# Eight more attention slots in the first batches; the second weight in four column groups, and the first half's output made one tile at a time

## The chip, the core and the metric

The kernel runs on one core of a Trainium2 chip. Time is the device time of one execution in microseconds (us). Five engines work side by side, each through its own queue in order: PE (TensorE, matrix products; PEld is its loading of the stationary operand), DVE (VectorE), ACT (ScalarE), POOL (GpSimd) and SP (SyncE, which here only issues transfers). A matrix product writes into PSUM, and DVE and ACT read it from there.

## What is computed

Causal attention with an extra bias for 8 batches of 8 heads (576 positions, head size 64), and behind it a feed-forward network over the 4608 tokens (512 to 2048 to 512):

```python
scores = scale * np.matmul(q, k.transpose(0, 1, 3, 2))
cum = np.cumsum(np.maximum(s, 0.0), axis=-1)
bias = -(cum[:, :, :, None] - cum[:, :, None, :])
scores = np.where(causal, -1000000000.0, scores + np.minimum(bias, 0.0))
attn = np.exp(scores - np.max(scores, axis=-1, keepdims=True))
attn = attn / (np.sum(attn, axis=-1, keepdims=True) + 1e-09)
x = np.matmul(attn, v)            # [B, H, S, D], then tokens x (H*D)
h = x @ w_in
g = np.where(h >= 1, h, np.where(h <= -1, 0.0, (h + 1) ** 2 / 4))
out = g @ w_out
```

The two weights come as 64-bit integers that hold doubles; the kernel decodes each to a 32-bit float, scales it by a power of two, and splits it into two 16-bit floats (a high and a low part). Every FFN product is then three 16-bit products.

## The kernel before

**Attention.** Work goes in jobs: a job is one pair of heads and one half of the positions. Half 0 (`hf` 0) has 320 positions in three row tiles (64, 128 and 128 rows), half 1 has 256 in two. A batch has eight jobs: four pairs of half 0, then four pairs of half 1. A job has eight slots (`att_slot(j, k)`, line 467): slot 0 converts q and k (`att_prep`), slots 2 to 7 make six units of scores (`scores`, lines 384 and 385 on PE, 390 on DVE, 401 on ACT), slot 3 issues the next job's loads on SP, and slot 7 makes the output of the job *before* (`att_out`, line 447 on PE, 458 and 459 for `x`). The weights of a row tile are split on POOL, ACT and DVE (lines 422 to 428) and transposed by a DMA on SP (line 429, tile `pt`); line 447 reads `pt`. The score tiles share two PSUM buffers.

**FFN.** A half of a batch goes through 16 row tiles of `w_in` (`ffn_h`, line 501: twelve products, three for each of four `kt`, where `kt` is the pair of heads), then ACT, DVE and POOL make `g` (lines 513 to 528), and `ffn_y` (line 540) adds each `g` into four output tiles `y0` to `y3` in PSUM, two row tiles behind. So the first product with `kt` = 3 needs the `x` of the last pair.

**Order.** The loop at line 605 has 512 steps, 32 for each half of a batch (two for each row tile). Each step issues one attention slot; in the first 32 steps every fourth step issues two. So from step 32 on, the slot counter `t` is 40 ahead of the step: step 32*q begins the FFN of half q (counted over all batches), and the `x` of its last pair comes from slot 32*q + 39, which was issued one step earlier. Attention ends 32 steps before the loop. A planner then sorts the instructions of each engine by priority (the order of issue, with leads of 6000 or 10000 for blocks under `high_priority`) and by its own simulated times; PE executes what it wrote strictly in that order.

**The second weight.** `Weights` (line 164) loads 16 chunks of 512 KB on SP (line 184), decodes each (lines 192 to 203), takes one scale over a group of chunks (`scale`, lines 208 to 216: ten small DVE instructions in a chain, with two PE products, lines 107 and 117, that use score buffers in PSUM) and splits the chunks (lines 221 to 229). For `w_out` there are two groups of eight chunks: 256 output columns each, a chunk being 256 rows by 256 columns. `w2_tasks` (line 591) issues two decode or split tasks at each of the first steps, with a lead of 6000. In steps 0 to 15 the FFN of the very first half only makes `h` and `g`; in steps 16 to 31 (lines 623 to 625) it makes `y`: first tiles 0 and 1 over all row tiles, then tiles 2 and 3, since the second group of `w_out` comes later. `batch_y` (line 294) makes one output scale per group and batch.

Of the kernel before, what the change touches and what calls it, by code (L numbers as in the profile page):

```python
# [14 lines left out]
AF = mybir.ActivationFunctionType  # L15
ALU = mybir.AluOpType
# [6 lines left out]
P = 128  # L23
NPAIR = H // 2
NKT = DM // P
NFT = DFF // P
# [25 lines left out]
WO_LAG = 2  # L52
# [21 lines left out]
def attention_ffn(ctx: ExitStack, tc: tile.TileContext, qT, kT, vT, s, w_in, w_out, yT):  # L74
    nc = tc.nc
    LOADQ, CUMQ, FIRSTQ = nc.sync, nc.scalar, nc.sync
    V, A, G, T = nc.vector, nc.scalar, nc.gpsimd, nc.tensor

    cp = ctx.enter_context(tc.tile_pool(name="cp", bufs=1))
    ap = ctx.enter_context(tc.tile_pool(name="ap", bufs=2))  # L80
    gp = ctx.enter_context(tc.tile_pool(name="gp", bufs=2))
# [75 lines left out]
    NC = 512  # L157
    WI = [cp.tile([P, 2, NC], F16, name=f"WI{c}") for c in range(NW)]
    WO = [cp.tile([P, 2, NC], F16, name=f"WO{c}") for c in range(NW + WO_LAG)]
# [4 lines left out]
    class Weights:  # L164
# [9 lines left out]
        def load(self, c, after=None):  # L174
            if c < NW:
                pool, tag, bufs = self.tags[c % len(self.tags)]
                self.raw[c] = pool.tile([P, NC, 2], I32, tag=tag, bufs=bufs, name=f"{self.name}r{c}")
                if after is not None:
                    V.tensor_copy(self.raw[c][:, 0, :1], after.bitcast(I32))
                src = self.src(c)  # L180
                dst = self.raw[c]
                if len(src.shape) == 4:
                    dst = dst.rearrange("p (j n) t -> p j n t", j=2)
                nc.sync.dma_start(dst, src)

        def decode(self, c):
# [46 lines left out]
        WO, WI, ((gp, "g", G_BUFS),), 1,  # L233
    )
    w2 = Weights(
        "wo", lambda c: w_out[c % 8 * 2 * P:(c % 8 + 1) * 2 * P, c // 8 * NC // 2:(c // 8 + 1) * NC // 2, :]
        .rearrange("(j p) n t -> p j n t", p=P),
        WO[WO_LAG:], WO, ((ap, "raw", 2), (gp, "x0", 2), (ap, "raw", 2)), 2,
    )
    a_in, b_out = w1.bound[0], w2.bound  # L240

# [1 line left out]
    vraw, csc, rcs, exs, hsc, rsc, usc, wsc, ubi, gsc, ysc, msc = ({} for _ in range(12))  # L243
# [25 lines left out]
    def batch_scales(b):  # L269
        m = msc[b]  # L270
        h = hsc[b] = ap.tile([P, 1], F32, tag="hs", name=f"hs{b}")
        V.tensor_scalar(h, m, a_in, 2.0 ** -27, ALU.mult, ALU.mult)

        r = rsc[b] = ap.tile([P, 1], F32, tag="r", name=f"r{b}")
        i = r.bitcast(I32)
        V.tensor_scalar(r, m, a_in, 2048.0, ALU.mult, ALU.mult)
        V.tensor_scalar(r, r, 1.0, None, ALU.max)
        V.reciprocal(r, r)
        V.tensor_scalar(r, r, 2.0 ** 14, None, ALU.mult)
        V.tensor_scalar(i, i, 23, None, ALU.logical_shift_right)  # L280
        V.tensor_scalar(i, i, 127, None, ALU.add)
        V.tensor_scalar(i, i, 1, 23, ALU.logical_shift_right, ALU.logical_shift_left)

        u = usc[b] = ap.tile([P, 1], F32, tag="us", name=f"us{b}")
        V.tensor_scalar(u, h, r, None, ALU.mult)
        w = wsc[b] = ap.tile([P, 1], F32, tag="ws", name=f"ws{b}")
        V.tensor_scalar(w, u, 2.0, None, ALU.mult)
        c = ubi[b] = ap.tile([P, 1], F32, tag="ub", name=f"ub{b}")
        V.tensor_scalar(c, r, 0.5, None, ALU.mult)
        g = gsc[b] = ap.tile([P, 1], F32, tag="gb", name=f"gb{b}")  # L290
        V.reciprocal(g, r)
        V.tensor_scalar(g, g, g, 2.0 ** 14, ALU.mult, ALU.mult)

    def batch_y(b, groups=(0, 1)):
        ysc.setdefault(b, {})
        for i in groups:
            y = ysc[b][i] = ap.tile([P, 1], F32, tag=f"ys{i}", name=f"ys{b}_{i}")
            V.tensor_scalar(y, gsc[b], b_out[i], 2.0 ** -28, ALU.mult, ALU.mult)
# [168 lines left out]
    def att_slot(j, k):  # L467

        if j < len(jobs):
            n, hf = jobs[j]  # L470
            if k == 0:
                att_prep(n, hf)
            if k == 1 and hf == 0:
                v_prep(n)
            if k == V_K and hf == 0:
                v_turn(n)
            if k >= 2:
                scores(n, *UNITS[hf][k - 2])
            if k == 3 and j + 1 < len(jobs):
                att_load(*jobs[j + 1])  # L480
            if k == 1 and j % (2 * NPAIR) == V_J and j // (2 * NPAIR) + 1 < B:
                load_v(j // (2 * NPAIR) + 1)
            if k == 5 and j + 1 < len(jobs) and jobs[j + 1][0] % NPAIR == 0 and jobs[j + 1][1] == 0:
                with tc.issue_after(ttr[0]):
                    batch_start(jobs[j + 1][0] // NPAIR)
        if k == OUT_K and 1 <= j <= len(jobs) and j != NPAIR:
            while j == len(jobs) and late:
                late.pop(0)()
            att_out(*jobs[j - 1])


    ffn_q, g4 = [], [None]
# [30 lines left out]
    def g_split(first=None):  # L523
        while to_split:
            g, u = to_split.pop()
            with tc.issue_after(first) if first is not None else ExitStack():
                A.copy(g[:, 0], u)  # L527
            G.tensor_tensor(g[:, 1], u, g[:, 0], ALU.subtract)  # L528

    ys = {}  # L530

    def ffn_y(b, hf, ft, g, ms=tuple(range(NKT))):
        h_off, N, _ = HALF[hf]
        if ft == 0:
            for m in ms:
                ys[b, hf, m] = ps_y.tile([P, 512], F32, tag=f"y{m}", name=f"y{b}_{hf}_{m}")
        for m in ms:
            c0 = ft % 2 * 2 * P + m % 2 * P
            for n, (wl, gl) in enumerate(((0, 0), (1, 0), (0, 1))):
                T.matmul(  # L540
                    ys[b, hf, m][:, :N], WO[8 * (m // 2) + ft // 2][:, wl, c0:c0 + P], g[:, gl],
                    start=(ft == 0 and n == 0), stop=(ft == NFT - 1 and n == 2),
                )
        if ft == NFT - 1:
            last = (b, hf) == (B - 1, len(HALF) - 1)
            for m in ms:
                tag, bufs = ("u", 4) if last and m >= 2 else ("o", O_BUFS)
                o = gp.tile([P, N], F32, tag=tag, bufs=bufs, name=f"o{b}_{hf}_{m}")
                y = ys[b, hf, m][:, :N]
                with tc.high_priority(offset=FFN_LEAD):  # L550
                    if last and m % 2:
                        V.tensor_scalar(o, y, ysc[b][m // 2], None, ALU.mult)
                    else:
                        A.activation(o, y, AF.Copy, scale=ysc[b][m // 2])
                (nc.sync if last and m % 2 else nc.scalar).dma_start(
                    yT[m * P:(m + 1) * P, b * S + h_off:b * S + h_off + N], o
                )

    def ffn_step(s, k):

        b, hf, ft = s // (2 * NFT), s // NFT % 2, s % NFT
        if k == 0:
            ffn_q.append((b, hf, ft, ffn_h(b, hf, ft)))
        elif len(ffn_q) > Y_LAG:
            ffn_y(*ffn_q.pop(0))
# [7 lines left out]
    for j in range(NPAIR):  # L573
        for k in range(8):
            if k % 2 == 0:
                c = 4 * j + k // 2
# [9 lines left out]
    for n in range(NW):  # L586
        c = n % 4 * 4 + n // 4
# [1 line left out]
    att_out(*jobs[NPAIR - 1])  # L589

    def w2_tasks():
        for g in range(2):
            for c in range(8 * g, 8 * g + 8):
                w2.decode(c)
                w2.load(c + 3)
                yield
            w2.scale(g, TINY)
            batch_y(0, (g,))
            for c in range(8 * g, 8 * g + 8):
                w2.split(c)  # L600
                yield

    t = 8 * NPAIR
    tasks = w2_tasks()
    for j in range(16 * NP):
        if j % 64 == 48 and j // 64 + 1 < B:
            batch_scales(j // 64 + 1)
            batch_y(j // 64 + 1)
        for _ in range(1 if j >= 2 * NFT else 1 + (j % 4 == 3)):
            att_slot(t // 8, t % 8)  # L610
            t += 1
        with tc.high_priority(offset=W2_LEAD):
            for _ in range(W2_RATE):
                next(tasks, None)
        if j >= 2 * NFT:
            ffn_step(j // 2, j % 2)
        elif j < NFT:
            ffn_step(j, 0)
        else:
            if j == NFT:  # L620
                with tc.high_priority(offset=FFN_LEAD):
                    g_split()
            m = 2 * (j // 8 % 2)
            for i in range(j % 8 * 2, j % 8 * 2 + 2):
                ffn_y(*ffn_q[i], ms=(m, m + 1))
            if j == 2 * NFT - 1:
                del ffn_q[:NFT]
    with tc.high_priority(offset=FFN_LEAD):
        g_split()
    while ffn_q:  # L630
        ffn_y(*ffn_q.pop(0))
# [28 lines left out]
```

## Time and profile before

| | us |
|---|---|
| median of 3 runs | 1171.36 (1170.36 to 1180.07) |
| the profiled execution | 1178.29 |
| its span, first to last instruction | 1176.2 |
| PE / DVE / ACT / POOL busy | 1009.5 / 892.6 / 746.0 / 691.0 |

The mean granted clock of PE is 0.967 of full speed. A busy PE is not a PE at its peak: matrix products are pipelined, and at a lower granted clock the same products are busy for longer. The table of stretches that is used below has, for each stretch of time, the busy time of PE, PEld, DVE, ACT and POOL with their instruction counts, then PE's granted clock, the share of the DMA engines and GB/s. A stretch's length less PE's busy time is PE's idle time.

### The profile page before, as it was taken

What the parts mean: (1) busy time and instruction counts of PE and PEld (TensorE: products, weight loads), DVE (VectorE), ACT (ScalarE), POOL (GpSimd) and SP (SyncE); (2) the same over time, 40 slices, a digit from 0 to 9 for tenths busy, and PEclk for the clock granted to TensorE, in tenths of its full rate; (3) what the DMA queues carried; (4) which work ended last, traced back from release to release, by engine and by line L of the source; (5) the groups of instructions that cost most, each with busy time, mean ns of one, the idle gap of its engine ahead of it and who ended that gap; (6) DMA issues with size and microseconds to landing.
All of it is one profiled execution on the core that took longest, in us unless ns stands there. A gap on an engine that the chain in (4) does not pass through costs nothing.

```text
span 1176.2 us, 25135 instructions
## 1 busy us (share of the span) xinstructions
PE 1009.5 (86%) x8470; PEld 776.6 (66%) x8470; DVE 892.6 (76%) x2404; ACT 746.0 (63%) x1719; POOL 691.0 (59%) x1169
## 2 busy tenths in 40 slices
PE   0234678699999999799998999899989999899998
PEld 0122345487767867587767867677768867686787
DVE  6879998778777877768777777778778877787633
ACT  4656677567656765767557665667557764777533
POOL 3876268676556664656546654656557564675522
PEclk9997999799998999999999999899999999899999
DMA  8885536867637773776638672876547753767310
GB/s 243 206 195 138 165 85 145 159 139 153 130 73 180 147 148 74 166 139 144 131 84 168 152 149 65 173 142 156 119 98 172 153 133 75 163 132 157 74 34 19
DMA packets 343081, 158.04 MB, mean 134 GB/s; under 512 B 291112, under 2 KB 324264, under 8 KB 342952
## 3 DMA queue, kind: packets, MB, share of 16 engines
q1 hardware_dynamic: 333248, 146.50, 59.0%
q10 hardware_dynamic: 9704, 9.93, 2.7%
q8 instruction: 67, 1.10, 0.4%
q14 instruction: 62, 0.51, 0.1%
HBM read 75.33 MB, written 9.73 MB: 72 GB/s over the span
## 4 chain that ended last, share of the span: by engine, by line
PE 42%; DVE 8%; DMA 5%; POOL 5%; issue 3%; ACT 1%; DVEq 0%; ACTq 0%; POOLq 0%
PE y L540 18%; PE h L501 17%; DMA pt<-pb 4%; PE px L447 3%; POOL pb L422 2%; DVE pb L428 2%; PE s L384 2%; PE s L385 2%; DMA vt<-vb 2%; POOL pb L425 1%; DVE p L390 1%; DVE K L339 1%; DVE h L516 1%; DVE Q L336 1%; POOL vb L350 1%
## 5 line engine op out<-in xcount | busy, mean ns | idle before, releaser
L501 PE MATMUL h<-x,WI 128*128 128x256 f16 (+1 forms) x3072 | 453.0, 292 | 23.4 <-DVE u L517 21.0
L540 PE MATMUL y<-g,WO 128*128 128x256 f16 (+1 forms) x3072 | 453.2, 291 | 17.3 <-POOL g L528 7.4
L501 PEld LDWEIGHTS <-WI 128*128 128x128 f16 x3072 | 292.3, 100 | 118.2 <-issue 28.2
L540 PEld LDWEIGHTS <-WO 128*128 128x128 f16 x3072 | 287.1, 99 | 108.7 <-issue 19.3
L528 POOL TENSOR_TENSOR g<-u,g 128x320 f16<-128x320 f32 (+1 forms) x256 | 199.2, 778 | 209.1 <-ACT g L527 203.9
L513 ACT ACTIVATE u<-h,ub,us 128x320 f32<-128x320 f32 (+1 forms) x256 | 149.3, 584 | 171.8 <-PE h L501 146.7
L401 ACT ACTIVATE p<-p,mn 64x64 f32<-64x64 f32 (+4 forms) x320 | 178.8, 559 | 113.6 <-DVE mn L390 96.4
L516 DVE SCALAR_TENSOR_TENSOR h<-h,ws,u 128x320 f32<-128x320 f32 (+1 forms) x256 | 133.0, 520 | 118.4 <-ACT u L513 117.9
L422 POOL TENSOR_SCALAR pb<-p,rs 64x128 f16<-64x128 f32 (+4 forms) x160 | 113.7, 711 | 152.2 <-DVE rs L418 118.6
L384 PE MATMUL s<-K,Q 128*128 128x288 f32 (+4 forms) x384 | 150.9, 395 | 43.8 <-DVE mn L390 33.3
L428 DVE SCALAR_TENSOR_TENSOR pb<-p,rs,pb 64x128 f16<-64x128 f32 (+4 forms) x160 | 135.8, 849 | 52.0 <-POOL pb L422 51.6
L425 POOL TENSOR_TENSOR pb<-p,pb 64x128 f16<-64x128 f32 (+4 forms) x160 | 165.0, 1032 | 9.2
L390 DVE CUSTOM_DVE_ANT_0 p<-s,mask 64x64 f32<-64x64 f32 (+4 forms) x320 | 134.8, 422 | 41.1 <-PE s L385 36.7
L517 DVE SCALAR_TENSOR_TENSOR u<-u,r,h 128x320 f32<-128x320 f32 (+1 forms) x256 | 130.2, 510 | 7.5
L423 ACT ACTIVATE p<-p,rs 64x64 f32<-64x64 f32 (+4 forms) x160 | 89.3, 559 | 67.2 <-DVE rs L418 60.6
L385 PE MATMUL s<-K,Q 68*128 68x288 f32 (+4 forms) x384 | 121.8, 319 | 9.8 <-ACT p L423 5.5
L447 PE MATMUL px<-pt,vt 128*64 128x256 f16 (+3 forms) x1536 | 87.7, 260 | 38.0 <-DMA pt<-pb 21.8
L384 PEld LDWEIGHTS s<-K,Q 128*128 128x128 f32 (+1 forms) x384 | 74.3, 194 | 68.2 <-DVE mn L390 42.4
L527 ACT CAST g<-u 128x320 f16<-128x320 f32 (+1 forms) x256 | 108.1, 422 | 10.6 <-DVE u L517 10.6
L447 PEld LDWEIGHTS <-vt 128*64 128x64 f16 x1536 | 73.2, 113 | 61.5 <-issue 40.3
L424 POOL TENSOR_SCALAR pb<-p 64x128 f16<-64x128 f32 (+4 forms) x160 | 90.9, 569 | 6.0 <-ACT p L423 2.9
L385 PEld LDWEIGHTS s<-K,Q 68*128 68x128 f32 (+1 forms) x384 | 75.8, 198 | 12.2 <-ACT p L423 5.9
(116 smaller groups left out, 961.4 us busy)
## 6 DMA issues: line engine op xcount, KB each, us to landing
rk<-in_k_dram SPq DMA_DIRECT2D x64, 288.0 KB
rq<-in_q_dram SPq DMA_DIRECT2D x64, 160.0 KB
rk<-in_k_dram SPq DMA_DIRECT2D x64, 160.0 KB
v<-in_v_dram SPq DMA_DIRECT2D x32, 288.0 KB
wir<-in_moe_w_in_dram SPq DMA_DIRECT2D x16, 512.0 KB
rq<-in_q_dram SPq DMA_DIRECT2D x64, 128.0 KB
wor<-in_moe_w_out_dram SPq DMA_DIRECT2D x16, 512.0 KB
out_dram<-o ACTq DMA_DIRECT2D x32, 160.0 KB
```

What stands on the lines that cost most here:

```text
L384: T.matmul(sc[:R, :c1 - c0], Q1[:, hd, qo:qo + R], K1[:, hd, c0:c1], start=True, stop=False)
L385: T.matmul(sc[:R, :c1 - c0], Q2[:KC, hd, qo:qo + R], K2[:KC, hd, c0:c1], start=False, stop=True)
L390: ttr[0] = V.tensor_tensor_reduce(out=Pt[:R, c0:c1], in0=sc[:R, :c1 - c0], in1=mask[:R, mo:mo + c1 - c0], scale=1.0, scalar=3.0e38 if mn i ...
L401: A.activation(Pt[:R, :W], Pt[:R, :W], AF.Exp, bias=m2[:R], scale=-1.0, accum_out=sums[n, i][:R, hd:hd + 1])
L425: G.tensor_tensor(los[1], pw, his[1], ALU.subtract)
L428: V.scalar_tensor_tensor(los[0], pv, rs[:R, :1], his[0], ALU.mult, ALU.subtract)
L447: T.matmul(px[hd * D:(hd + 1) * D, lo:N], VT[:, vl * NB + j, hd * D:(hd + 1) * D], PT[:, 4 * j + 2 * hd + pl, lo:], start=(m == 0), stop=( ...
L501: T.matmul(h[:, :N], WI[4 * kt + ft // 4][:, wl, ft % 4 * P:(ft % 4 + 1) * P], x[:, kt, xl], start=(n == 0), stop=(n == 3 * NKT - 1),)
L513: first = A.activation(u, h[:, :N], AF.Relu, bias=ubi[b], scale=usc[b]).ins
L516: V.scalar_tensor_tensor(h[:, :N], h[:, :N], wsc[b], u, ALU.mult, ALU.max)
L528: G.tensor_tensor(g[:, 1], u, g[:, 0], ALU.subtract)
L540: T.matmul(ys[b, hf, m][:, :N], WO[8 * (m // 2) + ft // 2][:, wl, c0:c0 + P], g[:, gl], start=(ft == 0 and n == 0), stop=(ft == NFT - 1 an ...
```

## The change

Three edits. First, `w_out` is cut into four groups of four chunks; a chunk is now 512 rows by 128 columns, so a group is exactly one output tile, each with its own scale, and `scale` and `batch_y` run for four groups. A contiguous run in memory is 128 columns of 8 bytes (1 KB) in place of 256 (2 KB). Second, the first half's `y` is made tile by tile: steps 16 to 19 make tile 0 over all 16 row tiles, 20 to 23 tile 1, and so on; each step has twelve products as before. Third, in steps 32 to 95 every eighth step issues one more attention slot, eight in all, so that from step 92 on the slot counter is 48 ahead of the step, and attention ends 40 steps before the loop.

```diff
@@ load
-                    dst = dst.rearrange("p (j n) t -> p j n t", j=2)
+                    dst = dst.rearrange("p (j n) t -> p j n t", j=src.shape[1])
@@ w2 = Weights(
-        "wo", lambda c: w_out[c % 8 * 2 * P:(c % 8 + 1) * 2 * P, c // 8 * NC // 2:(c // 8 + 1) * NC // 2, :]
+        "wo", lambda c: w_out[c % 4 * NC:(c % 4 + 1) * NC, c // 4 * P:(c // 4 + 1) * P, :]
         .rearrange("(j p) n t -> p j n t", p=P),
-        WO[WO_LAG:], WO, ((ap, "raw", 2), (gp, "x0", 2), (ap, "raw", 2)), 2,
+        WO[WO_LAG:], WO, ((ap, "raw", 2), (gp, "x0", 2), (ap, "raw", 2)), NKT,
@@ batch_y
-    def batch_y(b, groups=(0, 1)):
+    def batch_y(b, groups=range(NKT)):
@@ ffn_y
-            c0 = ft % 2 * 2 * P + m % 2 * P
+            c0 = ft % 4 * P
...
-                    ys[b, hf, m][:, :N], WO[8 * (m // 2) + ft // 2][:, wl, c0:c0 + P], g[:, gl],
+                    ys[b, hf, m][:, :N], WO[4 * m + ft // 4][:, wl, c0:c0 + P], g[:, gl],
...
-                        V.tensor_scalar(o, y, ysc[b][m // 2], None, ALU.mult)
+                        V.tensor_scalar(o, y, ysc[b][m], None, ALU.mult)
...
-                        A.activation(o, y, AF.Copy, scale=ysc[b][m // 2])
+                        A.activation(o, y, AF.Copy, scale=ysc[b][m])
@@ w2_tasks
-        for g in range(2):
-            for c in range(8 * g, 8 * g + 8):
+        for g in range(NKT):
+            for c in range(4 * g, 4 * g + 4):
                 w2.decode(c)
...
-            for c in range(8 * g, 8 * g + 8):
+            for c in range(4 * g, 4 * g + 4):
                 w2.split(c)
@@ the loop of steps
-        for _ in range(1 if j >= 2 * NFT else 1 + (j % 4 == 3)):
+        for _ in range(1 + (j % 4 == 3 if j < 2 * NFT else j % 8 == 3 and j < 6 * NFT)):
...
-            m = 2 * (j // 8 % 2)
-            for i in range(j % 8 * 2, j % 8 * 2 + 2):
-                ffn_y(*ffn_q[i], ms=(m, m + 1))
+            for i in range(j % 4 * 4, j % 4 * 4 + 4):
+                ffn_y(*ffn_q[i], ms=(j // 4 % 4,))
```

## The prediction

> **What bounds the kernel now.** I read the page first, then a table of stretches, then PE's timeline where PE is idle. The page's slices:
>
> ```profile
> PE   0234678699999999799998999899989999899998
> PEclk9997999799998999999999999899999999899999
> ```
>
> A slice is 29.4 us. The first eight (to about 235 us) have a partly idle PE; from then on PE is near full, with a dip about every 130 us, one for each batch. The stretches (after the times: PE, PEld, DVE, ACT, POOL busy; clock; DMA share; GB/s):
>
> ```profile
> 98.00:145.00 47.00, 24.91 (x133) 15.13 (x132) 43.41 (x97) 30.60 (x52) 22.46 (x24) 0.78 0.45 127
> 145.00:182.00 37.00, 27.34 (x189) 17.69 (x187) 33.68 (x74) 27.73 (x50) 24.79 (x24) 0.95 0.39 97
> 182.00:231.00 49.00, 36.01 (x267) 25.72 (x267) 40.46 (x112) 32.65 (x72) 36.27 (x55) 0.82 0.76 153
> 231.00:344.00 113.00, 110.56 (x956) 85.95 (x956) 86.28 (x237) 73.70 (x171) 69.11 (x115) 0.99 0.60 125
> ...
> 1126.00:1176.00 50.00, 46.28 (x417) 40.49 (x414) 16.74 (x35) 16.68 (x39) 11.49 (x17) 1.00 0.07 25
> ```
>
> So there are three stages. From 98 to 231 us (second weight, first half) DVE leads: 117.55 of 133 us. From 231 on PE is the bound. The tail is FFN alone, on PE alone. The six dips, where the FFN of half 1 of batches 1 to 6 begins:
>
> ```profile
> 344.00:364.00 20.00, 15.05 (x115) 11.38 (x113) 15.36 (x50) 13.26 (x39) 14.69 (x31) 0.83 0.88 180
> 475.00:500.00 25.00, 18.09 (x161) 14.21 (x160) 18.92 (x58) 17.62 (x49) 18.06 (x37) 0.93 0.84 181
> 607.00:632.00 25.00, 18.77 (x168) 14.75 (x166) 19.16 (x59) 17.11 (x50) 16.95 (x37) 0.93 0.97 182
> 738.00:758.00 20.00, 15.78 (x121) 12.07 (x120) 14.91 (x50) 12.46 (x37) 15.00 (x32) 0.83 0.89 190
> 869.00:889.00 20.00, 15.69 (x131) 12.28 (x129) 15.69 (x50) 13.04 (x38) 14.10 (x29) 0.91 0.90 185
> 1000.00:1020.00 20.00, 15.82 (x129) 11.68 (x126) 16.10 (x48) 15.13 (x43) 14.10 (x33) 0.83 0.91 180
> sum 130.00, PE 99.20 PEld 76.38 DVE 100.13 ACT 88.61 POOL 92.89; mean PE 16.53 PEld 12.73 DVE 16.69 ACT 14.77 POOL 15.48
> ```
>
> PE is idle there for 130.00 - 99.20 = 30.8 us. The missing clock, length times (1 - clock), is 3.4 + 1.75 + 1.75 + 3.4 + 1.8 + 3.4 = 15.5 us. Together 46.3 us. One dip on PE (the bracket is the idle time before the row and what ended it):
>
> ```profile
> 742.58 0.42 PE L384 MATMUL s<-K,Q 128*128 128x320 f32 x1 [0.42 <-DVE mn L390]
> 742.84 0.31 PE L385 MATMUL s<-K,Q 68*128 68x320 f32 x1
> 744.52 1.51 PE L447 MATMUL px<-pt,vt 128*64 128x256 f16 x30 [1.37 <-DMA pt<-pb]
> 745.97 0.24 PE L384 MATMUL s<-K,Q 128*64 128x64 f32 x1
> 747.30 0.21 PE L385 MATMUL s<-K,Q 68*64 68x64 f32 x1 [1.09 <-ACT p L423]
> 747.36 0.89 PE L501 MATMUL h<-x,WI 128*128 128x256 f16 x6
> ...
> 749.95 0.53 PE L384 MATMUL s<-K,Q 128*128 128x192 f32 x1 [1.33 <-DVE mn L390]
> ```
>
> The reader is to see a PE with nothing else to do. The `px` at 744.52 makes the last `x` of the half whose FFN is to begin; only behind it come the six products of L501 (`kt` = 3 for two row tiles, three each). The FFN is held by attention, and attention, in its narrow first units (64 and 192 columns), is a chain through DVE, ACT and DMA. Where the FFN has its `x`, the same thirty products come without a wait (second row; the first row is the first complete `h` of the first half 1, the end of the first stage):
>
> ```profile
> 231.17 2.72 PE L501 MATMUL h<-x,WI 128*128 128x256 f16 x12 [0.71 <-DVE u L517]
> ...
> 442.64 1.51 PE L447 MATMUL px<-pt,vt 128*64 128x256 f16 x30
> ```
>
> **The change, part by part.**
>
> *Eight more slots.* Until now the last `x` of a half is issued one step before its FFN; from step 92 on, nine steps before. Steps 32 to 96 take 231 to 344 us, 1.8 us each, so eight steps are 14 us, more than a whole dip. The dip's chain stays, but PE then still has products of the running half to put between. The first half 1 that profits from all eight begins at step 96, which is the dip at 344. So all six dips are reached. What stays? The stretch 231 to 344 is the measure of an FFN that has its `x`: idle 113 - 110.56 = 2.44 us and clock 1% = 1.13 us, so 3.1%, or 4.1 us in 130. That leaves 46.3 - 4.1 = 42.2 us. I keep back one wait: `px` for the transposed `pt`, about 1.37 us, since PE takes it in order and the planner may place it too early again; six times, 8.2 us. I take 34. The ends are 42 and 0 (all waits go along with attention); the row at 442.64 is why I stand near the upper one.
>
> *Where the slots go.* They are one job: its four loads and its `pt` transposes on SP, its two small transfers on ACT's queue, its POOL instructions, all 14 us sooner against the FFN. They fall into 231 to 344 and are missing in the tail. PE is full in both, so on PE this is zero. The cover on the others: in 231 to 344 lie eight jobs, so one more is at most an eighth: DVE 86.28 becomes at most 97 of 113 us, POOL 69.11 at most 78, DMA share 0.60 at most 0.68. None becomes the bound. On SP the four loads wait for their single buffers as before. The tail has no idle of its own to lose.
>
> *Two more scales.* The two of before:
>
> ```profile
> 133.07 0.15 DVE L208 TENSOR_REDUCE t_wo<-peak_wo 128x1 f32<-128x8 f32 x1
> 150.46 0.15 DVE L216 TENSOR_SCALAR r_wo<-r_wo 128x1 f32<-128x1 f32 x1
> 161.39 0.15 DVE L208 TENSOR_REDUCE t_wo<-peak_wo 128x1 f32<-128x8 f32 x1
> 177.46 0.27 PE L107 MATMUL row_wo<-ident,t_wo 128*1 128x128 f32 x1
> 177.77 0.28 DVE L109 TENSOR_REDUCE top_wo<-row_wo 1x1 f32<-1x128 f32 x1 [1.19 <-PE row_wo L107]
> 182.15 0.15 DVE L216 TENSOR_SCALAR r_wo<-r_wo 128x1 f32<-128x1 f32 x1
> ```
>
> Ten instructions, 0.15 us nearly all, 0.28 the longest: 1.6 us a set, 3.2 for two, on the bounding engine of that stage. The chain itself takes 17.4 us (133.07 to 150.46) and 20.8 us (161.39 to 182.15) and is hidden behind decodes and `h`; in the second, the PE product sat 16 us in PE's queue, behind `y` products that waited for chunks. Of `batch_y` there are 2 more in this stage and 14 later:
>
> ```profile
> L298 DVE TENSOR_SCALAR ys<-gb,bound_wo 128x1 f32<-128x1 f32 x16 | 2.8, 203 | 0.0
> L540 PE MATMUL y<-g,WO 128*128 128x320 f16 x1536 | 253.0, 308 | 6.9 <-POOL WO L227 3.1 <-ACT WO L221 3.0 <-DVE WO L229 0.8
> L192 ACT ACTIVATE WO<-wor 128x512 f32<-128x512 f32 x16 | 10.7, 674 | 14.8 <-DMA wor<-in_moe_w_out_dram 14.8
> q1 hardware_dynamic: 328, 0.61, 19.6%
> ```
>
> At 0.2 us: 0.4 us here; the 14 later lie under a PE that bounds. Cost of the part: 3.6 us.
>
> *Tile by tile.* Tile 0 needs four chunks and one scale, not eight; the last group to be split is half as large. At stake on PE are the 6.9 us of the L540 row; but DVE bounds, so the gain can be no more than DVE's idle time once `w_out` is done: 49 - 40.46 = 8.5 us in 182 to 231, where attention's last jobs are a chain. I take half, 4.3 us. The ends are 8.5 and -21, one more exposed chain of 20.8.
>
> *1 KB runs.* The q1 row (96 to 104 us, this load alone) has 328 packets in 0.196 * 16 * 8 us, 77 ns for each 2 KB. At worst a packet of 1 KB takes as long: 256 more in 16 engines, 1.2 us a chunk. The loads run ahead of the decodes; of ACT's 14.8 us of waiting most lies under a busy DVE. Between 0 and 4 us for the stage; I take 0, as DMA's share is 0.39 to 0.45.
>
> **Sum.** 34 + 4.3 - 3.6 = 34.7, say 35 us. The profiled execution took 1178.29 us, so 1143; that execution stands 6.9 us over the median of the runs, and against the median it is 1171.4 - 35 = 1136 us.
>
> **The clock, by row and by rule.** Three rows of the last dip, and the longest wait near any dip:
>
> ```profile
> 1000.00:1005.00 5.00, 3.20 (x42) 2.57 (x40) 4.36 (x16) 3.83 (x13) 3.34 (x8) 1.00 0.90 171
> 1005.00:1010.00 5.00, 2.62 (x26) 2.21 (x20) 3.99 (x11) 4.03 (x12) 4.18 (x10) 0.87 0.79 122
> 1010.00:1015.00 5.00, 5.00 (x21) 3.08 (x20) 3.74 (x15) 3.47 (x10) 2.94 (x7) 0.50 1.08 220
> ...
> 499.29 0.93 PE L540 MATMUL y<-g,WO 128*128 128x256 f16 x7 [2.62 <-POOL g L528]
> ```
>
> After ten microseconds in which PE was idle for 4.2, in pieces like those at 742 to 750, the clock is halved. So I count the 15.5 us as a consequence of the dips. The Trainium skill, "TensorE: Matmul & The Clock Gate", Part 1, says the clock halves after an idle window of about 3.4 us. No single gap of a dip is that long here (2.62 us is the longest), so by its letter the clock loss would not come from these gaps and the sum would be 15.5 us smaller; the rows above speak for the looser reading.
>
> **Rivals.**
> - *The clock loss has another cause and stays.* Only idle time is won: 35 - 15.5, so 1152 us. Against it: the low clock follows each dip. 0.10.
> - *Half.* The planner keeps the order around `px`, and the waits for `pt` and for `mn` (0.42 + 1.37 + 1.33 of 4.21 in the dip shown) largely stay in a thinner form: about half, 1171 - 17 = 1154 us. For it: PE's order is fixed beforehand. 0.13.
> - *The slots do nothing.* The dips belong to attention's chain and move along with it; only the stage at 98 to 231 is changed: 1171.4 - 4.3 + 3.6, some 1171 us. Against it: the row at 442.64. 0.07.
> - *Slower: four exposed scale chains.* Each group's chain waits in PE's queue behind `y` products for its chunks, as the second did (20.8 us), and decodes are too few to cover: three more such chains are 62 us, 1136 + 62 = 1198 us. It outweighs the gain from 35 us on and counts as slower from 47, so from the third chain. Against it: the first chain of before cost DVE nothing (43.41 of 47 us busy). 0.06.
> - *All of it.* The full 42 and the full 8.5 - 3.6: 1171 - 47 = 1124 us. 0.12.
>
> **Numbers.** My forecast, 1136, has the remaining 0.52. A difference of 1% (11.7 us) is about what can be told from none. The range 1118 to 1160 holds the forecast, "all", "half" and "clock" with their spread, and leaves out "nothing", "slower" and some of "half" at its upper edge, 0.18 together. Faster by over 1%: 0.52 + 0.12 + 0.10 + most of 0.13 = 0.84; within 1%: 0.10; slower: 0.06.
>
> **What would show it.** In the profile of after: at the six starts of half 1, no `px` with `x6` of L501 right behind it, PE idle under 2 us per 20 and clock 1.00; batches of about 124 us in place of 131; a last stretch of FFN alone that is about 15 us longer; four t_wo reductions with chains of 10 to 20 us; the first complete `h` of 256 columns still at 226 to 236 us. I am wrong if the dips stand at the same size, if DVE passes 95% between 231 and 344, or if the first stage grows by over 10 us.

## The result, and the profile after

| | before | changed |
|---|---|---|
| median of 4 runs, us | 1170.92 | 1141.07 (1137.98 to 1146.30) |
| ratio of the times | | 0.973 (0.967 to 0.980) |
| the profiled execution, us | 1178.29 | 1146.30 |
| its span, us | 1176.2 | 1144.5 |

The changed kernel is 2.7% faster, about 30 us; 35 were forecast (1136 us, range 1118 to 1160). On one chip beside some of the kernels below it was measured again, at 0.975 (0.972 to 0.978). A few executions run in a slower state (one of the kernel with early slots took 1338 us, at a granted clock of 0.761), and they are left out below.

First the page's slices of the changed kernel (28.6 us each):

```profile
PE   0234778699999999989998999999999999899998
PEclk9997989689999999999999999899999999999999
```

The first eight look as before. The dips behind them are shallower, not gone. The same in numbers: the table of stretches, at the same six places as in the prediction (from 11 us ahead of the first activation of half 1, and equally long):

```profile
340.00:360.00 20.00, 18.33 (x159) 14.10 (x158) 16.13 (x51) 15.08 (x43) 15.04 (x32) 0.91 0.91 191
467.00:492.00 25.00, 21.05 (x201) 16.89 (x199) 18.78 (x59) 18.85 (x53) 15.43 (x37) 1.00 0.86 181
591.00:616.00 25.00, 21.53 (x204) 17.22 (x202) 19.46 (x60) 19.33 (x56) 16.39 (x39) 1.00 0.84 183
719.00:739.00 20.00, 17.68 (x149) 13.57 (x149) 13.43 (x40) 13.57 (x37) 12.80 (x28) 0.83 0.68 155
842.00:862.00 20.00, 18.30 (x163) 13.99 (x162) 14.39 (x44) 15.22 (x42) 11.56 (x31) 0.91 0.87 182
970.00:990.00 20.00, 16.73 (x154) 13.05 (x152) 13.72 (x43) 13.97 (x38) 11.69 (x27) 0.91 0.61 140
sum 130.00, PE 113.62 PEld 88.83 DVE 95.91 ACT 96.03 POOL 82.91; mean PE 18.94 PEld 14.81 DVE 15.98 ACT 16.00 POOL 13.82
```

Idle time is 130.00 - 113.62 = 16.4 us (30.8 before). The missing clock is 1.8 + 3.4 + 1.8 + 1.8 = 8.8 us (15.5 before). Together 25.2 in place of 46.3: 21 us were won here, not 34. One of the six on PE's timeline:

```profile
719.27 0.93 PE L501 MATMUL h<-x,WI 128*128 128x256 f16 x7
...
720.34 0.40 PE L501 MATMUL h<-x,WI 128*128 128x256 f16 x2
...
722.52 1.51 PE L447 MATMUL px<-pt,vt 128*64 128x256 f16 x30
725.13 0.21 PE L384 MATMUL s<-K,Q 128*64 128x64 f32 x1 [1.11 <-DVE Q L336]
...
727.19 0.58 PE L501 MATMUL h<-x,WI 128*128 128x256 f16 x2 [0.47 <-ACT x L458]
...
728.32 0.50 PE L384 MATMUL s<-K,Q 128*128 128x192 f32 x1 [0.39 <-DVE mn L390]
```

The `px` at 722.52 no longer waits for its transposed `pt`. But it still stands inside the beginning of half 1 (the `h` of 256 columns begins at 719), `h` waits again for an `x` (0.47 us), and PE stands ahead of a score for line 336, DVE's conversion of q. So the slots brought far less than eight steps of lead here: this `px` starts 3.2 us behind the first `h` product of its half (719.27 to 722.52). In the kernel before it starts 6.9 us behind:

```profile
607.43 0.60 PE L501 MATMUL h<-x,WI 128*128 128x256 f16 x4
...
614.37 1.51 PE L447 MATMUL px<-pt,vt 128*64 128x256 f16 x30 [1.35 <-DMA pt<-pb]
```

Against its FFN the last `px` of the half has come 3.7 us sooner, where the prediction counted on 14. The first stage, in the stretches of the changed kernel, and the row in which it ends:

```profile
98.00:145.00 47.00, 26.19 (x138) 15.71 (x138) 44.06 (x104) 35.79 (x60) 26.55 (x24) 0.82 0.35 112
145.00:182.00 37.00, 29.28 (x197) 19.20 (x197) 32.88 (x90) 24.88 (x46) 23.91 (x25) 0.89 0.50 116
182.00:230.00 48.00, 36.77 (x255) 26.38 (x254) 37.19 (x114) 29.99 (x69) 34.86 (x50) 0.75 0.68 154
230.00:344.00 114.00, 113.66 (x984) 89.28 (x984) 92.43 (x254) 74.78 (x179) 71.61 (x126) 0.98 0.65 133
```

```profile
230.41 2.72 PE L501 MATMUL h<-x,WI 128*128 128x256 f16 x12 [0.22 <-DVE u L517]
```

DVE leads as before (114.1 of 132 us to 230), and the first complete `h` of half 1 comes at 230.41 against 231.17: four groups and four scales made the stage neither longer nor shorter. The gain lies behind it: 1144.5 - 230.4 = 914.1 us against 1176.2 - 231.2 = 945.0, 30.9 us, of which 21 lie at the six dips.

### The profile page after: what moved, and what is told of

Same layout as the page of the kernel before. It is cut to its first block, busy times and chain, and to the rows that moved or that the text cites. A ratio compares the mean times of both kernels' runs of the same rounds, so it can differ in the third digit from the quotient of the medians.

```text
span 1144.5 us, 25212 instructions
## 1 busy us (share of the span) xinstructions
PE 1001.2 (87%) x8474; PEld 775.8 (68%) x8474; DVE 884.1 (77%) x2440; ACT 739.4 (65%) x1719; POOL 686.2 (60%) x1169
## 4 chain that ended last, share of the span: by engine, by line
PE 61%; DVE 12%; POOL 8%; DMA 8%; issue 5%; ACT 5%; ACTq 0%; SPq 0%; DVEq 0%; POOLq 0%
PE h L501 25%; PE y L540 25%; PE px L447 4%; PE s L384 3%; DMA pt<-pb 3%; PE s L385 3%; DVE pb L428 2%; POOL pb L422 2%; DVE Q L336 1%; POOL pb L425 1%; DMA vt<-vb 1%; DVE p L390 1%; ACT p L401 1%; POOL g L528 1%; DVE h L516 1%
## 5 line engine op out<-in xcount | busy, mean ns | idle before, releaser
L501 PE MATMUL h<-x,WI 128*128 128x256 f16 (+1 forms) x3072 | 471.1, 292 | 24.6 <-DVE u L517 11.9
L540 PE MATMUL y<-g,WO 128*128 128x256 f16 (+1 forms) x3072 | 461.5, 290 | 14.1 <-POOL g L528 6.2
L540 PEld LDWEIGHTS <-WO 128*128 128x128 f16 x3072 | 290.4, 99 | 101.1 <-issue 12.4
L528 POOL TENSOR_TENSOR g<-u,g 128x320 f16<-128x320 f32 (+1 forms) x256 | 205.3, 802 | 155.0 <-ACT g L527 154.6
L422 POOL TENSOR_SCALAR pb<-p,rs 64x128 f16<-64x128 f32 (+4 forms) x160 | 102.1, 638 | 173.4 <-DVE rs L418 120.6
L447 PE MATMUL px<-pt,vt 128*64 128x256 f16 (+3 forms) x1536 | 83.7, 261 | 20.7 <-DVE mn L390 6.2
L424 POOL TENSOR_SCALAR pb<-p 64x128 f16<-64x128 f32 (+4 forms) x160 | 93.3, 583 | 9.3 <-ACT p L423 6.9
```

What stands on the lines that cost most here:

```text
L447: T.matmul(px[hd * D:(hd + 1) * D, lo:N], VT[:, vl * NB + j, hd * D:(hd + 1) * D], PT[:, 4 * j + 2 * hd + pl, lo:], start=(m == 0), stop=( ...
L501: T.matmul(h[:, :N], WI[4 * kt + ft // 4][:, wl, ft % 4 * P:(ft % 4 + 1) * P], x[:, kt, xl], start=(n == 0), stop=(n == 3 * NKT - 1),)
L540: T.matmul(ys[b, hf, m][:, :N], WO[4 * m + ft // 4][:, wl, c0:c0 + P], g[:, gl], start=(ft == 0 and n == 0), stop=(ft == NFT - 1 and n == 2),)
```

## The experiments

Theory A was that of the prediction: the last `x` of each half came too late, and the slots cure that. Rivals were that the four groups did it (B), that both are needed (C), or that it is the earlier end of attention that counts (C'). Each ratio below is to the kernel before on the same chip.

### The eight slots alone

```diff
 (the kernel before)
-        for _ in range(1 if j >= 2 * NFT else 1 + (j % 4 == 3)):
+        for _ in range(1 + (j % 4 == 3 if j < 2 * NFT else j % 8 == 3 and j < 6 * NFT)):
```

> The kernel before with the eight extra slots alone; the second weight and the order of the first half's output stay as they were. Theory A (the last x of each half comes too late; the slots cure the six dips): about 1141 us, 30 us under the 1171 us of before, the dips at the starts of half 1 down to under 2.5 us of idle time each. Rival B (the four column groups and the tile-by-tile order do it, by ending the first stage earlier): about 1171 us. Rival C (both are needed, since the slots lean on an earlier end of the first stage): 1155 us or so.

Measured: 1131.36 us, ratio 0.963 (0.960 to 0.967). That is theory A, by 10 us more than it foretold, and more than the whole change gains. The stretches at the six places, in this kernel:

```profile
338.00:358.00 20.00, 18.01 (x143) 13.35 (x142) 15.67 (x48) 15.02 (x42) 13.94 (x33) 0.83 0.87 173
461.00:486.00 25.00, 22.74 (x216) 18.53 (x215) 20.06 (x64) 19.78 (x57) 17.30 (x40) 1.00 0.93 192
...
952.00:972.00 20.00, 17.68 (x172) 14.19 (x171) 15.69 (x52) 15.73 (x43) 12.88 (x31) 1.00 0.76 153
sum 130.00, PE 121.08 PEld 96.71 DVE 105.60 ACT 103.45 POOL 90.24; mean PE 20.18 PEld 16.12 DVE 17.60 ACT 17.24 POOL 15.04
```

Idle 8.9 us, and a lower clock only in the first (3.4 us): 12.3 of 46.3 are left, 34 are won at the dips. A rest of 6 to 9 us (the whole gain is 39.7 to 42.8) is won between them. But the lead of 14 us is not in this trace either:

```profile
589.32 0.60 PE L501 MATMUL h<-x,WI 128*128 128x256 f16 x4
...
591.79 1.51 PE L447 MATMUL px<-pt,vt 128*64 128x256 f16 x30
```

The last `px` starts 2.5 us behind the first `h` product of its half, at five of the six starts (5.5 us at the first); before it was 6.9 to 7.4 us at all six. A shift of 4.5 us was enough: `px` hardly waits for `pt` there (0.3 us in all six places), and PE has products of half 0 to put between the scores of the next job.

### The four groups alone, and with the old order of the output

The changed kernel with the old slot line; then, besides, with the old two passes of two tiles:

```diff
 (the changed kernel without the slots; the second run only)
-            for i in range(j % 4 * 4, j % 4 * 4 + 4):
-                ffn_y(*ffn_q[i], ms=(j // 4 % 4,))
+            m = 2 * (j // 8 % 2)
+            for i in range(j % 8 * 2, j % 8 * 2 + 2):
+                ffn_y(*ffn_q[i], ms=(m, m + 1))
```

> The changed kernel without the eight extra slots: four column groups, tile by tile. Theory A: no difference, 1171 us within 4 us, all six dips as before, the first complete h of 256 columns at 230 us. Rival B: about 1141 us. If the two further scales cost what I counted for them and nothing comes back: 1175 us.

> As the run before it (four column groups, no extra slots), but the first half's output in two passes of two tiles, as in the kernel before, so that tiles 0 and 1 need two scales first. If attention's chain ends the first stage: the same time as with tile by tile, within 3 us. If the order of the output sets the end of that stage: 5 to 10 us slower.

Measured: 1168.84 us, 0.9954 (0.9927 to 0.9980), and 1168.51 us, 0.9949 (0.9924 to 0.9973). Rival B falls: the groups give some 5 us, not 30, and the order of the first half's output gives nothing. The dips are all there in the first of the two:

```profile
sum 130.00, PE 103.25 PEld 81.18 DVE 101.42 ACT 89.33 POOL 87.92; mean PE 17.21 PEld 13.53 DVE 16.90 ACT 14.89 POOL 14.65
```

Idle is 26.75 us (30.8 before), and the six rows have clocks of 0.83, 0.93, 0.86, 0.91, 0.74 and 0.83, so 19 us are missing there (15.5 before): together 45.8 in place of 46.3. Where the 5 us come from is not settled: the first complete `h` comes at 229.5 us in the one and 225.4 in the other, with the same time in the end.

### The slots at batch 3

```diff
-        for _ in range(1 if j >= 2 * NFT else 1 + (j % 4 == 3)):
+        for _ in range(1 + (j % 4 == 3 if j < 2 * NFT else j % 8 == 3 and 12 * NFT <= j < 16 * NFT)):
```

> The kernel before with the eight extra slots in steps 192 to 255 (batch 3) in place of steps 32 to 95. Theory A: the dips of batches 1 and 2 stay (about 7.5 us with their clock loss), that of batch 3 shrinks in part, those of batches 4 to 6 are cured: a gain of 3.5 sixths of 30, so about 1153 us, between 1150 and 1158. Rival C' (what counts is that attention ends one job sooner, with a longer tail of FFN alone): the whole 30 us, 1141. Rival B: 1171 us.

Measured: 1148.70 us, 0.977 (0.974 to 0.981). Its stretches:

```profile
344.00:364.00 20.00, 15.78 (x133) 12.36 (x132) 15.47 (x49) 13.40 (x39) 13.96 (x31) 0.91 0.88 185
474.00:499.00 25.00, 18.44 (x156) 14.62 (x155) 18.97 (x57) 17.63 (x49) 17.89 (x37) 0.90 0.86 181
609.00:634.00 25.00, 21.22 (x190) 16.82 (x189) 19.21 (x62) 18.76 (x55) 16.54 (x38) 0.93 1.00 192
733.00:753.00 20.00, 18.79 (x181) 15.10 (x180) 16.09 (x54) 16.23 (x45) 13.54 (x33) 1.00 0.95 195
854.00:874.00 20.00, 19.36 (x184) 15.39 (x182) 15.56 (x49) 16.21 (x46) 13.00 (x30) 1.00 1.04 198
981.00:1001.00 20.00, 17.74 (x173) 14.25 (x171) 15.58 (x51) 15.55 (x43) 12.77 (x31) 1.00 0.77 156
```

The dips ahead of the slots stay (4.2 and 6.6 us idle, clock 0.91 and 0.90), the one among them is partly filled (3.8 us), those behind are gone or small (1.2, 0.6 and 2.3 us, clock 1.00). Attention ends sooner here too (the last `x` begins 60.5 us ahead of the end of the span, 61.5 us with the slots in steps 32 to 95), and yet the gain is 25.5 us where those slots gave 42.8 on the same chip. So rival C' falls: a dip is cured only when the slots lie ahead of it. The time was 1.3 us under the lower end that I gave, but 3.5 sixths of 42.8, the gain that the slots really have, is 25.0 us.

### What four groups cost once the slots are there

The changed kernel gains less than the slots alone, though the groups without the slots cost nothing. First the two kernels again, on one chip:

> The changed kernel, unaltered, beside the next three on one chip. All theories: 1138 to 1146 us.

> The kernel before with the eight extra slots alone, again, beside the changed kernel. If the four column groups cost something once the slots are there: 8 to 12 us under the changed kernel (1131). If the 10 us between the two so far were two chips: equal within 3 us.

Measured: 1143.07 us, 0.975 (0.972 to 0.978), and 1132.96 us, 0.966 (0.963 to 0.969). The difference of 10 us is real. Two suspects: the fourteen further instructions of `batch_y` in the later batches (D), or the first stage (E). So the slots alone with fourteen such instructions, and the changed kernel with one instruction per later batch for all four scales:

```diff
 (the slots alone, and)
             batch_y(j // 64 + 1)
+            for i in (2, 3):
+                y = ap.tile([P, 1], F32, tag=f"ys{i}", name=f"ys{j // 64 + 1}_{i}")
+                V.tensor_scalar(y, gsc[j // 64 + 1], b_out[i - 2], 2.0 ** -28, ALU.mult, ALU.mult)
```

```diff
 (the changed kernel, and)
-            self.bound = [cp.tile([P, 1], F32, name=f"bound_{name}{g}") for g in range(groups)]
+            self.bounds = cp.tile([P, groups], F32, name=f"bound_{name}")
+            self.bound = [self.bounds[:, g:g + 1] for g in range(groups)]
...
+        if b:
+            y = ap.tile([P, NKT], F32, tag="ysb", name=f"ysb{b}")
+            V.tensor_scalar(y, w2.bounds, gsc[b], 2.0 ** -28, ALU.mult, ALU.mult)
+            ysc[b] = {i: y[:, i:i + 1] for i in range(NKT)}
+            return
```

> The eight slots alone, and for each later batch two more small DVE instructions of the kind of line 298 (output scales that nobody reads): fourteen in all, 2.8 us of DVE time, as four groups have them. Theory D (these fourteen instructions are what four groups cost in the later batches, since the planner, which counts them, orders PE's scores and products of each batch differently around them): as the changed kernel from 230 us on, so about 1140 us, batches of 125 us. Rival E (what costs is the first stage with its four scales, which leaves attention further behind): 1131 us, as with the slots alone, batches of 122 us.

> The changed kernel (four groups, tile by tile, eight slots), but the output scales of each later batch are made by one DVE instruction of four columns in place of four of one column: one fewer than the kernel before had. Theory D: the 8 to 10 us come back, about 1131 us, batches of 122 us. Rival E: 1140 us.

Measured: 1149.18 us, 0.979 (0.976 to 0.982), and 1130.81 us, 0.964 (0.961 to 0.967). So theory D holds against E: fourteen instructions of 0.2 us cost 16 us beside the slots alone, where 9 were foretold (1140 less 1131), and with one instruction per batch in place of four the changed kernel wins 12.3 us and four groups cost nothing. In the tile view of `ys`, of the first of the two kernels, they are these (duration least, median, most in ns; first and last start):

```profile
L611 DVE TENSOR_SCALAR ys<-gb,bound_wo x14: 193/203/204, 214.4 to 959.4; 128x1 f32<-128x1 f32 x14
```

2.8 us of DVE work would hardly cost 16 by themselves on an engine that is idle for a fifth of the time. Their place is the suspect. DVE's timeline in the changed kernel:

```profile
581.85 0.57 DVE L298 TENSOR_SCALAR ys<-gb,bound_wo 128x1 f32<-128x1 f32 x4
582.45 0.82 DVE L336 SCALAR_TENSOR_TENSOR Q<-rq,Q 64x640 fp32r<-64x640 f32 x1
583.30 0.82 DVE L339 TENSOR_TENSOR K<-rk,K 64x640 fp32r<-64x640 f32 x1
```

They stand right ahead of lines 336 and 339 of a batch's first job, which the chain of its narrow scores begins with. And the planner counts them: of the 16161 matrix products and weight loads in PE's program, the kernel with the fourteen instructions has the last 14774 in exactly the order of the changed kernel. The slots alone have another order, with scores and `h` products exchanged around each start of a batch. The traces show it as well: in the two slower kernels the last `px` of a half starts 3.2 us behind the first `h` product of its half (6.3 us at the first start), in the two faster ones 2.5 us (5.5 at the first).

### The same fourteen instructions in another place

```diff
 (the changed kernel)
-            batch_y(j // 64 + 1)
+        if j % 64 == 60 and j // 64 + 1 < B:
+            with tc.issue_after(ttr[0]):
+                batch_y(j // 64 + 1)
```

> The changed kernel with all its work, the four output scales of each later batch as four instructions, but issued twelve steps later and held on DVE behind a score instruction of that time, so that they no longer stand right ahead of line 336 for the first job of a batch. Theory F (not the 2.8 us of the fourteen instructions cost the time, but their place: ahead of the chain that starts a batch's attention, where the planner then sorts PE's scores later): 1130 to 1134 us, as with one instruction. Rival G (the four instructions cost it wherever they stand): 1143 us, as the changed kernel.

Measured: 1125.51 us, 0.958 (0.955 to 0.961). That speaks for theory F, though 4.5 us under the least time it gave, and it is the fastest kernel of all. Its gain over the kernel before is 48.4 us, that of the changed kernel, with the same work, 29.6 us on another chip. Rival G falls. The tile view of `ys` has all 32 instructions, and the stretches at the six places:

```profile
L298 DVE TENSOR_SCALAR ys<-gb,bound_wo x32: 190/200/210, 128.5 to 1011.0; 128x1 f32<-128x1 f32 x32
```

```profile
586.00:611.00 25.00, 23.89 (x227) 19.56 (x227) 21.01 (x69) 19.84 (x58) 18.73 (x40) 1.00 0.89 198
706.00:726.00 20.00, 19.45 (x187) 15.70 (x187) 16.52 (x54) 16.25 (x47) 14.71 (x34) 1.00 0.89 202
826.00:846.00 20.00, 19.53 (x187) 15.72 (x187) 16.47 (x54) 16.26 (x47) 14.40 (x34) 1.00 0.96 204
...
sum 130.00, PE 122.16 PEld 98.27 DVE 103.28 ACT 102.31 POOL 91.00; mean PE 20.36 PEld 16.38 DVE 17.21 ACT 17.05 POOL 15.17
```

Idle 7.8 us in 130, and where the dips at 719 and 591 were, 0.5 and 1.1. What is not separated: whether it is DVE's delay of 0.6 us ahead of line 336 that costs, or the order of PE that the planner makes of it. Holding the instructions back changes both (the last `px` is at 2.5 us again), and no run changes PE's order alone. So the cost of these instructions is shown; that their place costs it through the chain, and not through what the planner happens to make of any such change, is not.

### How many slots, and where

```diff
 (the kernel before; three runs)
+        for _ in range(1 + (j % 4 == 3 if j < 2 * NFT else j % 16 == 3 and j < 6 * NFT)):    # 4 slots
+        for _ in range(1 + (j % 4 == 3 and j < 6 * NFT)):                                    # 16 slots
+        for _ in range(1 + (j % 2 == 1 and j < 2 * NFT)):                                    # 8, in steps 0 to 31
```

> The kernel before with four extra slots (steps 35, 51, 67, 83) in place of eight. Theory A: the last x is ready 7 us before its FFN in place of 14; a dip lasts 10 to 25 us with 4 to 7 us of idle time, so most of it is filled: 1136 to 1145 us. If it takes the whole eight slots: 1150 to 1160 us.

> The kernel before with sixteen extra slots in steps 32 to 95 (every fourth step). Theory A: the dips are gone with eight, so no more is won: 1128 to 1135 us, with a tail of FFN alone that is another 12 us longer. If each slot of lead is worth something by itself: 1110 us or less. If the lead runs into a buffer: over 1140 us.

> The kernel before with the eight extra slots in steps 0 to 31 (two slots every second step) in place of 32 to 95. DVE bounds there and gets one more job, at most 11 us. Theory A: the dips of batches 1 to 6 are cured as well, the first stage ends up to 8 us later, of which the x that is then ready for half 1 gives some back: 1130 to 1140 us. If the wait for x at 200 to 231 us was what held the first stage: under 1128 us.

Measured: 1136.81 us, 0.970 (0.966 to 0.974); 1133.03 us, 0.966 (0.963 to 0.968); 1139.64 us, 0.971 (0.968 to 0.974). Four slots give most of it (37.1 us), and sixteen give what eight give (40.9 us). But sixteen also brought no more lead than eight. The last `x` begins 61.7 us ahead of the end of the span, against 61.5 with eight, where 12 us more were foretold. The last `px` of a half starts 2.5 us behind the first `h` product with four, eight and sixteen slots alike, at five of the six starts. And of PE's 16161 products and weight loads the last 13237 stand in the same order with eight and with sixteen. So what a longer lead would be worth is not shown, and what holds attention back is open. In the early place the gain is smaller (34.3 us). The stage of that last kernel, to be held against 40.46 us of DVE in the kernel before:

```profile
182.00:231.00 49.00, 33.98 (x253) 23.63 (x251) 35.85 (x105) 29.84 (x65) 32.84 (x47) 0.82 0.59 126
231.00:344.00 113.00, 108.22 (x934) 84.84 (x933) 89.19 (x244) 73.37 (x174) 70.46 (x120) 0.97 0.65 134
```

DVE is less busy and PE not more: more slots issued there do not make attention faster, and the stretch behind, full before (110.56), now has 4.8 us of idle time.

## Why the prediction was right, point by point

**The time: right, in part by luck.** 35 us were forecast and 30 came, but out of other terms. The slots alone give 39.7 to 42.8 us in place of 34, the groups alone 5.3 in place of 0.7, and a term that was put at nothing took 12 to 16 us back. At the dips of the changed kernel 21 us were won of the 42 that were to be had; that is what the rival "half" said of them, with waits for `mn` that stay. The other 10 us behind 230 us were won between the dips, and no term of the sum stood for them.

**The dips and their cause: right in kind; the lead of 14 us did not come.** Six dips at the starts of half 1, cured in the order in which the slots reach them, by the runs with the slots alone and with the slots at batch 3. The size, 34 us, is what the slots alone win at these places (46.3 to 12.3). The bound of 42 was nearer to the whole gain of the slots, 39.7 us (1172.62 to 1132.96). Of the 14 us that eight steps were to bring, the last `px` gained 4.5 us against its FFN with the slots alone and 3.7 us in the changed kernel.

**The wait held back for `px`: right sum, wrong item.** I kept 8.2 us because PE would go on waiting for `pt`. With the slots alone 12.3 us stay at the dips, just the 4.1 and 8.2 of the sum, but not as waits for `pt`. The `px` of half 1 (256 columns) waited for `pt` in the kernel before and hardly does in the changed one (first line before, second changed, both over the whole execution):

```profile
L447 PE MATMUL px<-pt,vt 128*64 128x256 f16 x576 | 40.3, 280 | 23.1 <-DMA pt<-pb 21.1 <-DVE pb L428 1.8 <-DVE mn L390 0.2
L447 PE MATMUL px<-pt,vt 128*64 128x256 f16 x576 | 39.5, 284 | 3.4 <-DMA pt<-pb 3.0 <-DVE mn L390 0.3
```

At the six places of the changed kernel PE waits 5.5 us for `mn`, 3.1 for line 336, 2.5 for an `x` and 0.8 for `pt`. That, and the lower clock behind it, is what stays.

**`batch_y`, "the 14 later lie under a PE that bounds": the term that was mis-sized.** Taken as 0; measured 16.2 us beside the slots alone, and 12.3 us in the changed kernel against one instruction per batch. The cover I named was PE, but at the start of a batch PE waits for attention's chain, and there the instructions stood. On one chip the steps are: slots alone -39.7, four groups with one such instruction per batch -2.2 more, four instructions +12.3; the changed kernel has -29.6 (1172.62 to 1143.07). The groups alone, without the slots, have the instructions too and are 5.3 us faster than the kernel before, so there the cost does not show; why, no run tells.

**Where the slots go: right.** Between 230 and 344 us DVE is busy 92.43 of 114 us (81%; at most 97 of 113 was said), POOL 71.61, DMA share 0.65. The tail of FFN alone is longer: the last `x` is begun at 1083.4, 61.1 us ahead of the end of the span, against 1125.9 and 50.3; 15 us more was said, it is 10.8:

```profile
L459 DVE SCALAR_TENSOR_TENSOR x<-px,ex,x x64: 464/506/552, 62.9 to 1083.4; 128x320 f16<-128x320 f32 x32, 128x256 f16<-128x256 f32 x32
```

**Two more scales and tile by tile: right in sum for the stage, not in the parts.** +3.6 and -4.3 were said; the stage ends 0.8 us earlier. The chains of the scales take 18.8 us (112.5 to 131.3), 29.7 (128.5 to 158.3), 28.0 (147.5 to 175.5) and 20.0 (164.3 to 184.3), so two are longer than the 10 to 20 us that were said. They overlap, and PE waits for them (line 212) only 4.0 us in all, so the rival that ended slower did not come. That the tile order gives part of the gain was not so: the run in pairs has the same time, and PE's waits in the row of L540, 6.9 us before, are 10.1 us (last line below). The groups' own 5 us showed in the whole time, not in the stage, and have no explanation here.

```profile
L208 DVE TENSOR_REDUCE t_wo<-peak_wo x4: 138/146/148, 112.5 to 164.3; 128x1 f32<-128x4 f32 x4
...
L216 DVE TENSOR_SCALAR r_wo<-r_wo x4: 141/146/154, 131.3 to 184.3; 128x1 f32<-128x1 f32 x4
...
L540 PE MATMUL y<-g,WO 128*128 128x320 f16 x1536 | 254.9, 306 | 10.1 <-POOL g L528 2.9 <-DVE WO L229 2.8 <-DVE top_wo L212 1.9
```

**1 KB runs: right.** In 96 to 104 us, with this load alone, 660 packets take 0.232 * 16 * 8 = 29.7 us of the engines for 0.64 MB; before, 328 packets took 25.1 us for 0.61 MB. That is an eighth more time for each byte. The 77 ns of the prediction are a little low for a packet of 2 KB, since 32 packets in each window are of 4 bytes (9 ns each): without them it is 84 ns for 2 KB and 47 ns for 1 KB. ACT waits 11.5 us for these chunks (14.8 before).

```profile
q1 hardware_dynamic: 660, 0.64, 23.2%
```

**The clock: right, by the rows.** Where the dips go, the clock loss goes (15.5 us before, 3.4 with the slots alone), so the rival in which it stays is out. In the changed kernel 8.8 us stay at the dips, and the first stage loses more than before (0.81 in 98 to 231 us, against 0.84), so that over the whole execution the mean clock is 0.968, against 0.967. A dip of the changed kernel shows how little it takes:

```profile
719.00:724.00 5.00, 5.00 (x58) 3.91 (x57) 2.29 (x9) 3.42 (x8) 2.55 (x6) 1.00 0.57 131
724.00:729.00 5.00, 2.68 (x18) 2.01 (x17) 3.74 (x10) 1.70 (x6) 2.91 (x8) 0.82 0.57 131
729.00:734.00 5.00, 5.00 (x22) 3.38 (x20) 4.14 (x16) 3.45 (x11) 2.77 (x7) 0.50 1.10 219
```

The longest single gap there is the 1.11 us at 725.13, yet the clock falls in the stretch in which PE is idle for half the time (mean 0.82) and is halved in the next. The Trainium skill, "TensorE: Matmul & The Clock Gate", Part 1, tells of an idle window of about 3.4 us; read as one unbroken gap, it does not agree with this trace.

**The signs.** The first stage, DVE between 231 and 344 us and the longer tail came as said. At the six starts PE is idle for 2.5 us per 20 (under 2 were said), and four of them have a clock under 1.00; the batches take 126 us on average (from 351 to 981), where 124 were said.

## What to carry to other kernels

Where a consumer's stage begins with a short idle time of the bounding engine, look at how far ahead its producer was issued: a small lead (here four to eight slots) is worth most of the dip, its clock loss included. Then read from the trace how much of the lead arrived: eight slots were to bring 14 us and brought 4.5, and eight more brought nothing further. When a small instruction is added ahead of a chain that starts a stage, do not count it by its duration alone: fourteen instructions of 0.2 us cost 12 to 16 us ahead of a batch's first scores, and held back until later they cost nothing that could be seen. And run the parts of a change alone: this one held a part that gives 40 us, one that gives 5, and a by-product that took 12 to 16 back.

## What was not expected of the hardware

The granted clock of PE fell to 0.50 behind gaps of which none was longer than 1.11 us, in a stretch in which PE was busy for 2.68 of 5 us. Halving the contiguous run of the weight's loads to 1 KB cost the DMA engines an eighth more time for the same bytes (29.7 us for 0.64 MB against 25.1 us for 0.61 MB), not twice as much.
